# Full-size tail products, full two-batch tiles and all of q loaded ahead, in the ramp of a fused linear attention and two expert layers

## The chip, the cores and the metric

The kernel runs on one core of a Trainium2 chip, in one launch. The time is that of the device from start to end, in microseconds (us), as the median of several runs. One more execution was taken with the hardware profiler; its rows are the ones shown below. PE is TensorE, the matrix engine; DVE is VectorE, ACT is ScalarE, POOL is GpSimd, and SP is the engine that issues most of the DMA transfers.

## What is computed

```python
# q, k, v: (4, 8, 576, 64), float32
kv = np.einsum('bhsd,bhse->bhde', k, v)
out = np.einsum('bhsd,bhde->bhse', q, kv)
rms = np.sqrt(np.mean(out * out, axis=-1, keepdims=True) + 1e-06)
x = (out / rms * g_norm)            # then as 2304 tokens of 512
# first layer, 512 -> 2048 -> 512
h = np.maximum(x @ w_in, 0.0)
x = h * h @ w_out
# second layer, four experts of 1024
p = domain_probs / (domain_probs.sum(-1, keepdims=True) + 1e-09)
for e in range(4):
    out2 += p[:, e:e + 1] * (np.maximum(x @ w1[e], 0.0) @ w2[e])
```

Attention here has no softmax: for each head, a 64 x 64 matrix kv is summed over the 576 positions of its batch, and each token's q is multiplied by it. w_in and w_out come as 64-bit numbers.

## The kernel before

**Tiles.** Two heads share one product of 128 x 128, of which only the two 64 x 64 blocks on the diagonal are wanted. There are 4 batches x 4 head pairs, so 16 such products, called k0 to k15 (batch 0 has k0 to k3, and so on). A batch has 576 = 4 x 128 + 64 positions: four full chunks of 128 rows and a tail of 64. The 2304 tokens make 18 tiles of 128; since 576 is 4.5 tiles, tiles 4 and 13 hold tokens of two batches. The tokens are also taken in five blocks, of 512, 512, 512, 512 and 256 (`BLK`, `j` in the code).

**Units of work.** The program is a list of named units, run through in order; each writes its instructions for all engines. `RAMP` is the hand-written list for the attention and the start of the first layer; `rest()` makes the list behind it.

- `k` (`att_kv`): PE multiplies k and v of a pair, four full chunks (L286) and then the tail (L287), which lies on half of the 128 rows of its tile. The two blocks are copied to a matrix `kvd`, which is zero elsewhere, one by ACT (L289) and one by DVE (L290). It then issues the load of the pair eight further on. There are eight `kvd`, so k8 writes over that of k0.
- `o` (`att_a`, `att_out`): PE multiplies a tile of q by the four `kvd` of its batch (L301). A tile with two batches does so in two halves of 64 tokens. ACT squares the result (L310), DVE sums the squares of each head (L311).
- `c` (`att_c`): DVE and ACT make the factors 1/rms for a group of two or three tiles (L325 to L330), and DVE multiplies the products by them into `xn` (L333).
- `b` (`att_b`): PE transposes `xn` (L344); ACT scales it by g (L348) and rounds it to `hi` (L148), POOL makes the low part `lo` (L149). Both stand in `x`, one tile for each block. Products of the layers are sums of three products of such parts.
- `w` (`split_w`, `narrow`) takes the next piece of weights and loads the one two further on into the freed place (there are two). Each slice of the first layer has four pieces; the first four are called w0 to w3 here. ACT takes an absolute value (L173), DVE takes five steps (L175, L179, L182, L187, L188). `y` (`split_narrowed`) lets ACT round (L231) and POOL do two operations (L232, L233).
- `f` (`g1`): a slice's first product of the layer for a block (L377); ACT then takes ReLU (L382), the square (L384) and the rounding, POOL the low part. `g` (`g2a`) is the second product (L398), which DVE adds up in an accumulator `acc`, one for each block.

**Order.** Each engine works through its own list of instructions in order; a framework builds these lists from the units and may set independent instructions of different units in another order. An instruction waits on semaphores for what it reads, and for the last use of the place that it writes. Products on PE go to eight banks. A float32 product of 128 x 128 shows as two passes (rows "x8" for four chunks).

**Places and loads.** SP issues the loads in its order; the framework has eight semaphores for DMA transfers, so a transfer waits until that eight before it has landed. k and v of the first six pairs go to places that later are the accumulators of blocks 1 to 3, the others to two places of their own; tails have two places, tiles of q four. Loads for later pairs and tiles are issued as places come free.

Of the kernel before, what the change touches and what calls it, by code (L numbers as in the profile page):

```python
# [43 lines left out]


# [75 lines left out]
def fused_kernel(ctx, tc, kvm, kvt, qt, g2, probs, w64, w32, out):  # L121
# [170 lines left out]

    def att_out(t, ss):
        po = ps.tile([P, 512], F32, tag="ps", name=f"po{t}")
        q = q_in.pop(t)
# [12 lines left out]
        load_q(t + NQ)  # L308
        sq = tmp.tile([P, 512], F32, tag="tmp", name=f"sq{t}")
        nc.scalar.activation(out=sq, in_=po, func=AF.Square)  # L310
# [1 line left out]
        return po
# [7 lines left out]
    def att_c(g):  # L320
# [10 lines left out]
        for m, t in enumerate(group):  # L331
            xn = tmp.tile([P, 512], F32, tag="tmp", name=f"xn{t}")
            nc.vector.tensor_tensor(  # L333
                out=xn.rearrange("p (h d) -> p h d", h=H),
                in0=po_t.pop(t).rearrange("p (h d) -> p h d", h=H),
                in1=st[:, 3, m, :].unsqueeze(2).to_broadcast([P, H, D]), op=ALU.mult,
            )
# [224 lines left out]
    with ExitStack() as actx:  # L562
# [11 lines left out]
        load_kv(0)
        load_kv(1)
        load_w(0)
        load_kv(2)
        load_kv(3)
        load_q(0)
        load_q(1)  # L580
        load_w(1)
        load_q(2)
        load_q(3)
# [55 lines left out]
```

## Time and profile before

| | |
|---|---|
| median of 3 runs | 1217.11 us (1216.68 to 1217.98) |
| profiled execution | 1214.15 us |
| its span | 1212.4 us |
| PE busy | 1193.0 us, 98% |
| DVE busy | 765.8 us, 63% |
| POOL busy | 500.3 us, 41% |
| ACT busy | 439.9 us, 36% |

The span runs from the first to the last instruction of the profiled execution. Busy time is that of instructions alone, without waits. PE is the bound over most of the span; in the first 50 us the DMA engines and DVE are as busy as PE is. In that stretch a time line by engine tells more than a sum: what an instruction waits for is in square brackets behind it.

### The profile page before, as it was taken

The page shows a single profiled execution, that of the slowest core. Times are in us where ns is not written, and L with a number is a line of the kernel's source. Part 1 is how long each engine was busy: PE and PEld are TensorE (multiplying, and loading weights), DVE is VectorE, ACT ScalarE, POOL GpSimd, SP SyncE. Part 2 cuts the span into 40 slices and gives each one's busy share as a digit, 9 for nine tenths or more (in the row PEclk, how much of TensorE's full clock was granted, in tenths as well). Part 3 has the DMA queues.
Part 4 walks back from the last instruction along what each step waited for, and adds up shares of the span by engine and source line. Part 5 has one row for each costly group of instructions (what it writes and reads, how often), then busy time and mean ns, then how long its engine had stood idle before and what let it go on. Part 6 is the DMA issues. An engine that isn't in the chain of part 4 may idle for free.

```text
span 1212.4 us, 14974 instructions
## 1 busy us (share of the span) xinstructions
PE 1193.0 (98%) x5768; PEld 1003.2 (83%) x5768; DVE 765.8 (63%) x1177; ACT 439.9 (36%) x798; POOL 500.3 (41%) x390
## 2 busy tenths in 40 slices
PE   7999999999999999999999999999999999999998
PEld 6888788888888888888888888888788888888887
DVE  5968845545546466566666566656876666666655
ACT  4575444434445563222222222322433232323220
POOL 3556635445546675222323222323645242434310
PEclk9999999999999999999999999999999999999999
DMA  8611201111111101110111101111131121111101
GB/s 317 233 42 53 88 18 53 35 36 53 44 44 45 59 20 33 37 36 35 36 53 35 52 35 35 36 52 35 52 123 70 35 70 35 67 38 63 42 1 70
DMA packets 22247, 70.20 MB, mean 58 GB/s; under 512 B 2720, under 2 KB 2720, under 8 KB 22176
## 3 DMA queue, kind: packets, MB, share of 16 engines
q1 hardware_dynamic: 21888, 69.22, 16.7%
q8 instruction: 45, 0.74, 0.2%
q14 instruction: 26, 0.21, 0.1%
q10 hardware_dynamic: 288, 0.04, 0.0%
HBM read 64.52 MB, written 4.72 MB: 57 GB/s over the span
## 4 chain that ended last, share of the span: by engine, by line
PE 91%; DVE 5%; DMA 1%; issue 1%; POOL 1%; ACT 1%; SPq 0%; DVEq 0%; POOLq 0%; ACTq 0%
PE p L529 32%; PE p L377 18%; PE p L398 15%; PE pa L484 7%; PE pd L484 7%; PE pc L484 7%; PE pb L484 4%; PE po L301 1%; DVE u L179 1%; DMA kvs<-in_kvm 1%; DVE u L182 1%; DVE k L188 1%; DMA raw<-in_w 1%; DVE u L175 0%; PE pt L344 0%
## 5 line engine op out<-in xcount | busy, mean ns | idle before, releaser
L529 PE MATMUL p<-b,hh 128*128 128x512 f32 x1152 | 382.8, 390 | 0.5 <-ACT hh L516 0.5
L529 PEld LDWEIGHTS p<-b,hh 128*128 128x128 f32 x1152 | 216.3, 188 | 45.0 <-ACT hh L516 0.7
L539 DVE SCALAR_TENSOR_TENSOR acc<-p,p_sb,acc 128x512 f32<-128x512 f32 x270 | 199.4, 745 | 49.7 <-PE p L529 49.1
L529 PE MATMUL p<-b,hl 128*128 128x512 f32 x576 | 224.6, 390 | 0.0
L377 PE MATMUL p<-x,a 128*128 128x512 f32 (+1 forms) x960 | 204.3, 368 | 0.0
L377 PEld LDWEIGHTS p<-x,a 128*128 128x128 f32 x960 | 167.7, 189 | 30.4 <-PE po L301 0.2
L398 PE MATMUL p<-hh,b 128*128 128x512 f32 (+1 forms) x640 | 189.7, 370 | 0.0
L149 POOL TENSOR_TENSOR a<-raw,a 128x512 fp32r<-128x512 f32 x64 | 85.6, 1338 | 232.8 <-DVE pd L511 149.0
L405 DVE TENSOR_TENSOR acc<-p,acc 128x512 f32<-128x512 f32 (+1 forms) x140 | 87.9, 633 | 142.6 <-PE p L398 141.7
L149 POOL TENSOR_TENSOR b<-raw,b 128x512 fp32r<-128x512 f32 x64 | 82.1, 1303 | 188.0 <-ACT b L148 186.7
L149 POOL TENSOR_TENSOR hl<-s,hh 128x512 fp32r<-128x512 f32 (+1 forms) x80 | 97.9, 1226 | 120.0 <-ACT hh L148 116.7
L398 PEld LDWEIGHTS p<-hh,b 128*128 128x128 f32 x640 | 116.5, 189 | 20.2 <-ACT hh L148 0.4
L529 PEld LDWEIGHTS p<-b,hl 128*128 128x128 f32 x576 | 108.2, 188 | 21.4 <-DVE hl L517 0.2
L398 PE MATMUL p<-hl,b 128*128 128x512 f32 (+1 forms) x320 | 118.3, 370 | 2.4 <-POOL hl L149 2.4
L484 PE MATMUL pc<-o,a 128*128 128x512 f32 x384 | 97.6, 390 | 2.1 <-DVE u L499 2.1
L484 PE MATMUL pa<-o,a 128*128 128x512 f32 x384 | 97.6, 389 | 0.0
L484 PE MATMUL pd<-o,a 128*128 128x512 f32 x384 | 97.4, 389 | 0.0
L149 POOL TENSOR_TENSOR a<-w,a 128x512 fp32r<-128x512 f32 x64 | 85.0, 1328 | 25.3 <-ACT a L148 25.3
L148 ACT ACTIVATE a<-raw 128x512 fp32r<-128x512 f32 x64 | 40.1, 629 | 140.6 <-DMA raw<-in_w 109.2
L382 ACT ACTIVATE r<-p 128x512 f32<-128x512 f32 (+1 forms) x80 | 44.1, 552 | 122.2 <-PE p L377 121.7
L484 PEld LDWEIGHTS pc<-o,a 128*128 128x128 f32 x384 | 72.0, 188 | 17.5 <-DVE u L499 2.5
L484 PEld LDWEIGHTS pd<-o,a 128*128 128x128 f32 x384 | 72.1, 188 | 15.0
(92 smaller groups left out, 1477.3 us busy)
## 6 DMA issues: line engine op xcount, KB each, us to landing
raw<-in_w SPq DMA_DIRECT2D x96, 512.0 KB, 3.7
kvm<-in_kvm SPq DMA_DIRECT2D x10, 512.0 KB, 4.0
q<-in_qt SPq DMA_DIRECT2D x18, 256.0 KB, 4.6
out<-acc SPq DMA_DIRECT2D x18, 256.0 KB, 3.5
kvs<-in_kvm SPq DMA_DIRECT2D x6, 512.0 KB, 7.2
kvt<-in_kvt SPq DMA_DIRECT2D x4, 256.0 KB, 6.0
p_raw<-in_probs ACTq DMA_DIRECT2D x1, 36.0 KB, 4.8
g_sb<-in_g ACTq DMA_DIRECT2D x1, 0.5 KB, 4.3
```

Source lines behind the costliest of these rows:

```text
L148: nc.scalar.activation(out=hi, in_=full, func=AF.Copy)
L149: nc.gpsimd.tensor_tensor(out=lo, in0=full, in1=hi.bitcast(F32), op=ALU.subtract)
L179: nc.vector.scalar_tensor_tensor(out=u, in0=high, scalar=0xC0000000, in1=u, op0=ALU.bitwise_and, op1=ALU.bitwise_or)
L182: nc.vector.scalar_tensor_tensor(out=u.bitcast(F32), in0=k, scalar=1.125 * 2.0**-15, in1=u.bitcast(F32), op0=ALU.is_ge, op1=ALU.mult,)
L188: nc.vector.scalar_tensor_tensor(out=k.bitcast(F32), in0=low, scalar=2.0**-52, in1=k.bitcast(F32), op0=ALU.mult, op1=ALU.mult)
L377: nc.tensor.matmul(pt[:, :n], w, x, start=(i == 0), stop=(i == len(steps) - 1))
L382: nc.scalar.activation(out=r[:, :n], in_=pt[:, :n], func=AF.Relu)
L398: nc.tensor.matmul(pt[:, :n], w, h, start=(i == 0), stop=(i == len(steps) - 1))
L405: nc.vector.tensor_tensor(out=a, in0=pt[:, :n], in1=a, op=ALU.add)
L484: nc.tensor.matmul(pr[bank], x, y, start=(m == 0 and not more), stop=(m == len(steps) - 1), skip_group_check=more,)
L529: nc.tensor.matmul(pt, h, w, start=(i == 0), stop=(i == len(steps) - 1))
L539: nc.vector.scalar_tensor_tensor(out=a, in0=pt, scalar=pe, in1=a, op0=ALU.mult, op1=ALU.add)
```

## The change

- **Loads.** All of k, v of pairs 0 to 9 and all of q are loaded ahead, in the order of a new list `LOADS`. k and v of the first eight pairs go to two places that later are `x` of blocks 2 and 3; q goes to the five accumulators' places. The later pairs still have two places of their own.
- **Tails.** The tail of a batch is one tile of 128 rows for all four pairs, of which the lower 64 rows are set to zero once by POOL; the load fills the upper 64. The tail's product is a full one. There are two such tiles; that of batch b + 2 is loaded behind the last pair of batch b.
- **Two-batch tiles.** Tiles 4 and 13 are multiplied in full by the `kvd` of each of their two batches, into two banks; squares and `xn` take 64 rows from each.
- **Copies.** Both blocks of `kvd` are copied by ACT.
- **Order.** The first `w` and `y` of `RAMP` stand behind k3 and o1, no longer ahead of k0 and behind k1.

```diff
+LOADS = """
+k0 k1 q0 k2 k3 w0 q1 q2 q3 w1 k4 q4 k5 q5 k6 q6 k7 q7 k8 q8 k9 q9 q10 q11 q12 q13 q14 q15 q16 q17
+""".split()
 RAMP = """
-w k0 k1 y k2 k3 o0 o1 k4 c0 o2 o3 b0 k5 k6 b1 c1 b3 w b2 k7 y w o4 o5 y k8 o6 w k9 f0.0.0 y
+k0 k1 k2 k3 w o0 o1 y k4 c0 o2 o3 b0 k5 k6 b1 c1 b3 w b2 k7 y w o4 o5 y k8 o6 w k9 f0.0.0 y
...
-    NQ = 4
+    NKV = 2
+    stage = [xp.tile([P, 4, 2, NCK, P], F32, tag="xs", name=f"kvs{i}", bufs=4) for i in range(2)]
+    NSTAGE = 8
...
+    def load_tails(b):
+        if b < B:
+            nc.sync.dma_start(out=tails[b % 2][:STAIL], in_=kvt[b])
     def load_kv(i):
...
-        if c == 0:
-            tails[b] = attp.tile([P, 2, 2, P], F32, tag="kvt", name=f"kvt{b}")
-            nc.sync.dma_start(out=tails[b], in_=kvt[b])
+        if c == 0 and b < 2:
+            load_tails(b)
...
-        q_in[t] = attp.tile([P, NPAIR, P], F32, tag="q", name=f"q{t}", bufs=NQ)
-        nc.sync.dma_start(out=q_in[t], in_=qt[t])
+        j, m = divmod(t, 4)
+        if m == 0:
+            q_in[j] = accp.tile([P, BLK[j][1] // P, NPAIR, P], F32, tag=f"acc{j}", name=f"q{j}")
+        nc.sync.dma_start(out=q_in[j][:, m], in_=qt[t])
     def att_kv(i):
...
-        tl = tails[b][c % 2 * STAIL : (c % 2 + 1) * STAIL, c // 2]
+        tl = tails[b % 2][:, c]
...
         nc.scalar.activation(out=kd[:D, :D], in_=pk[:D, :D], func=AF.Copy)
-        nc.vector.tensor_copy(kd[D:, D:], pk[D:, D : 2 * D])
-        load_kv(i + NSTAGE + 2)
+        nc.scalar.activation(out=kd[D:, D:], in_=pk[D:, D:P], func=AF.Copy)
+        if i >= NSTAGE:
+            load_kv(i + NKV)
+        if c == NPAIR - 1:
+            load_tails(b + 2)
     def att_out(t, ss):
...
         while done < P:
             b, r = divmod(t * P + done, S)
-            n = min(P - done, S - r)
+            rows = slice(done, done + min(P - done, S - r))
+            po = ps.tile([P, 512], F32, tag="ps", name=f"po{t}_{b}")
             for c in range(NPAIR):
                 nc.tensor.matmul(
-                    po[done : done + n, c * P : (c + 1) * P],
-                    q[:, c, done : done + n],
-                    kvd[(b * NPAIR + c) % NKVD],
+                    po[:, c * P : (c + 1) * P], q[:, c, :], kvd[(b * NPAIR + c) % NKVD],
                     start=True, stop=True,
                 )
-            done += n
-        load_q(t + NQ)
-        nc.scalar.activation(out=sq, in_=po, func=AF.Square)
+            nc.scalar.activation(out=sq[rows], in_=po[rows], func=AF.Square)
+            parts.append((rows, po))
+            done = rows.stop
...
+        tails += [small.tile([P, NPAIR, 2, P], F32, name=f"kvt{i}", bufs=1) for i in range(2)]
+        for t in tails:
+            nc.gpsimd.memset(t[STAIL:], 0.0)
```

`att_c` multiplies each of a tile's parts by its rows of the factors; the identity for the transposes is made behind the memsets.

The lists of two engines differ at one place between k8 and f0.0.1. In the names below, `pk8` is the product of k8, `po6_1` that of tile 6, `p1_0_0_0` and `p1_0_0_1` are f0.0.0 and f0.0.1, `k0_2` and `k0_3` the absolute values of w2 and w3, `sq4` the squares of tile 4, `b0` and `a0` the rounded weights. On PE, before:

```order
L286 MATMUL pk8_394<-kvm8_166 128x128 x4
L287 MATMUL pk8_394<-kvt2_168 128x128
L301 MATMUL po6_403<-kvd4_97,q6_252 128x128
L301 MATMUL po6_403<-kvd5_98,q6_252 128x128
L301 MATMUL po6_403<-kvd6_99,q6_252 128x128
L301 MATMUL po6_403<-kvd7_100,q6_252 128x128
L286 MATMUL pk9_423<-kvm9_178 128x128 x4
L287 MATMUL pk9_423<-kvt2_168 128x128
L377 MATMUL p1_0_0_0_433<-x0_80,a0_146 128x512 x12
L377 MATMUL p1_0_0_1_455<-x0_80,a0_146 128x512 x12
```

and after:

```order
L298 MATMUL pk8_384<-kvm8_147 128x128 x4
L320 MATMUL po6_1_396<-kvd4_99,q1_139 128x128
L320 MATMUL po6_1_396<-kvd5_100,q1_139 128x128
L320 MATMUL po6_1_396<-kvd6_101,q1_139 128x128
L320 MATMUL po6_1_396<-kvd7_102,q1_139 128x128
L298 MATMUL pk9_413<-kvm9_151 128x128 x4
L395 MATMUL p1_0_0_0_425<-x0_82,a0_197 128x512 x12
L395 MATMUL p1_0_0_1_447<-x0_82,a0_197 128x512 x12
L299 MATMUL pk8_384<-kvt0_103 128x128
L299 MATMUL pk9_413<-kvt0_103 128x128
```

The two tails (L287, now L299) have moved behind f0.0.0 and f0.0.1. On ACT, at the same place, before:

```order
L231 ACTIVATE a0_146<-u0_1_326 128x512
L173 ACTIVATE k0_2_356<-raw0_2_156 128x512
L310 ACTIVATE sq4_378<-po4_367 128x512
L310 ACTIVATE sq5_388<-po5_381 128x512
L289 ACTIVATE kvd0_93<-pk8_394 64x64
L231 ACTIVATE b0_147<-u0_2_358 128x512
L310 ACTIVATE sq6_410<-po6_403 128x512
L289 ACTIVATE kvd1_94<-pk9_423 64x64
```

and after:

```order
L240 ACTIVATE a0_197<-u0_1_319 128x512
L301 ACTIVATE kvd0_95<-pk8_384 64x64
L302 ACTIVATE kvd0_95<-pk8_384 64x64
L301 ACTIVATE kvd1_96<-pk9_413 64x64
L302 ACTIVATE kvd1_96<-pk9_413 64x64
L182 ACTIVATE k0_2_348<-raw0_2_207 128x512
L324 ACTIVATE sq4_359<-po4_0_360 64x512
L324 ACTIVATE sq4_359<-po4_1_366 64x512
L324 ACTIVATE sq5_373<-po5_1_374 128x512
L240 ACTIVATE b0_198<-u0_2_350 128x512
```

The copies from `pk8` and `pk9`, now two each, stand ahead of the absolute value of w2 (L173, now L182) and of the squares. On SP, the loads around w2 (`raw0_2`), before:

```order
L268 DMA kvm6_142<-in_kvm 128x1024
L268 DMA kvm7_144<-in_kvm 128x1024
L164 DMA raw0_2_156<-in_w64 128x512
L271 DMA kvt2_168<-in_kvt 128x512
L268 DMA kvm8_166<-in_kvm 128x1024
```

and after:

```order
L278 DMA kvm9_151<-in_kvm 128x1024
L290 DMA q2_149<-in_qt 128x512 x3
L290 DMA q3_156<-in_qt 128x512 x4
L290 DMA q4_161<-in_qt 128x512 x2
L268 DMA kvt0_103<-in_kvt 64x1024
L173 DMA raw0_2_207<-in_w64 128x512
L173 DMA raw0_3_325<-in_w64 128x512
```

w2 has moved behind k9, the last nine tiles of q and the tail of batch 2.

## Rows read from the trace of the kernel before

**Rows 1.** The page: busy time, share of the span, instructions.

```profile
PE 1193.0 (98%) x5768; PEld 1003.2 (83%) x5768; DVE 765.8 (63%) x1177; ACT 439.9 (36%) x798; POOL 500.3 (41%) x390
```

**Rows 2.** What PE waited for: us in total, times, longest.

```profile
PE pk L286 <- DMA kvs<-in_kvm: 6.1, 2, 5.0
PE po L301 <- DVE kvd L290: 2.6, 2, 1.9
...
PE pc L484 <- DVE u L499: 2.1, 1, 2.1
```

**Rows 3.** PE's time line: start, busy us, operation, count, wait.

```profile
4.96 2.07 PE L286 MATMUL pk<-kvs 128*128 128x128 f32 x8 [4.96 <-DMA kvs<-in_kvm]
...
26.15 1.06 PE L286 MATMUL pk<-kvm 128*128 128x128 f32 x8
27.14 0.48 PE L287 MATMUL pk<-kvt 64*128 64x128 f32 x2
27.55 1.36 PE L301 MATMUL po<-kvd,q 128*64 128x128 f32 x14
...
34.80 5.74 PE L377 MATMUL p<-x,a 128*128 128x512 f32 x24
40.38 1.05 PE L286 MATMUL pk<-kvm 128*128 128x128 f32 x8
...
58.17 2.05 PE L301 MATMUL po<-kvd,q 128*128 128x128 f32 x16
...
64.36 1.58 PE L301 MATMUL po<-kvd,q 128*64 128x128 f32 x16
65.88 5.75 PE L377 MATMUL p<-x,a 128*128 128x512 f32 x24
...
73.72 1.95 PE L301 MATMUL po<-kvd,q 128*128 128x128 f32 x16
75.50 0.60 PE L344 MATMUL pt<-ident,xn 128*128 128x128 f32 x4
```

**Rows 4.** The chain that ended last, first 17 us: start, us, what.

```profile
2.10 6.34 DMA raw<-in_w
...
8.46 7.82 DMA kvs<-in_kvm
```

**Rows 5.** DVE's time line in the ramp, columns as for PE.

```profile
34.63 0.68 DVE L182 SCALAR_TENSOR_TENSOR u<-k,u 128x512 f32<-128x512 f32 x1
...
36.52 1.70 DVE L188 SCALAR_TENSOR_TENSOR k<-raw,k 128x512 f32<-128x512 uint32 x1
...
44.15 0.69 DVE L188 SCALAR_TENSOR_TENSOR k<-raw,k 128x512 f32<-128x512 uint32 x1
44.88 1.29 DVE L333 TENSOR_TENSOR xn<-po,st 128x512 f32<-128x512 f32 x2
...
46.45 1.28 DVE L311 TENSOR_REDUCE st<-sq 128x8 f32<-128x512 f32 x2
...
61.94 1.47 DVE L188 SCALAR_TENSOR_TENSOR k<-raw,k 128x512 f32<-128x512 uint32 x1
```

**Rows 6.** POOL's time line: last additions of w1 and of slice 1's first piece.

```profile
32.22 1.33 POOL L233 TENSOR_TENSOR a<-u,k 128x512 fp32r<-128x512 f32 x1
...
63.56 1.28 POOL L233 TENSOR_TENSOR a<-u,k 128x512 fp32r<-128x512 f32 x1 [0.69 <-DVE st L325]
64.80 1.26 POOL L149 TENSOR_TENSOR x<-xg,x 128x512 fp32r<-128x512 f32 x1
```

**Rows 7.** ACT's time line: the absolute value of w2, the copy from pk8.

```profile
29.36 0.66 ACT L173 ACTIVATE k<-raw 128x512 f32<-128x512 f32 x1
...
32.52 0.22 ACT L289 ACTIVATE kvd<-pk 64x64 f32<-64x64 f32 x1 [0.71 <-PE pk L287]
```

**Rows 8.** The kvd copies (L290) on DVE in 34.63 to 63.41: busy, granted clock.

```profile
34.63:63.41 28.78, 1.59 (x7) 1.00 0.69 233
```

**Rows 9.** What DVE waited for between 34.6 and 63.45 us.

```profile
DVE st L311 <- ACT sq L310: 0.9, 1, 0.9
```

More of the change, by code (lines that the diff above doesn't have):

```diff
@@ L133, in fused_kernel @@
     NKVD = 2 * NPAIR
-    NQ = 4
-    kvd = []
+    NKV = 2
+    kvd, tails = [], []
     p_sb = const.tile([P, NTT, E], F32, name="p_sb")
+    stage = [xp.tile([P, 4, 2, NCK, P], F32, tag="xs", name=f"kvs{i}", bufs=4) for i in range(2)]
+    NSTAGE = 8
     x_t = [
@@ L252, in operands @@
             split(*(a[:, x, 2:4] for x in range(2)), st[n])
-    kv_in, q_in, tails, stage, st_t, po_t, att_mid = {}, {}, {}, [None], {}, {}, {}
-    NSTAGE = 6
+    kv_in, q_in, st_t, po_t, att_mid = {}, {}, {}, {}, {}
+    def load_tails(b):
+        if b < B:
+            nc.sync.dma_start(out=tails[b % 2][:STAIL], in_=kvt[b])
     def load_kv(i):
@@ L262, in load_kv @@
         if i < NSTAGE:
-            if i % 2 == 0:
-                stage[0] = accp.tile([P, 2, 2, NCK, P], F32, tag=f"acc{i // 2 + 1}", name=f"kvs{i}")
-            m = stage[0][:, i % 2]
+            m = stage[i // 4][:, i % 4]
         else:
-            m = attp.tile([P, 2, NCK, P], F32, tag="kvm", name=f"kvm{i}")
+            m = attp.tile([P, 2, NCK, P], F32, tag="kvm", name=f"kvm{i}", bufs=NKV)
         nc.sync.dma_start(out=m, in_=kvm[b, c])
-        if c == 0:
-            tails[b] = attp.tile([P, 2, 2, P], F32, tag="kvt", name=f"kvt{b}")
-            nc.sync.dma_start(out=tails[b], in_=kvt[b])
+        if c == 0 and b < 2:
+            load_tails(b)
         kv_in[i] = m
@@ L289, in att_kv @@
         nc.scalar.activation(out=kd[:D, :D], in_=pk[:D, :D], func=AF.Copy)
-        nc.vector.tensor_copy(kd[D:, D:], pk[D:, D : 2 * D])
-        load_kv(i + NSTAGE + 2)
+        nc.scalar.activation(out=kd[D:, D:], in_=pk[D:, D:P], func=AF.Copy)
[3 more added lines that the diff above has]
+            load_tails(b + 2)
     def att_out(t, ss):
-        po = ps.tile([P, 512], F32, tag="ps", name=f"po{t}")
-        q = q_in.pop(t)
+        q = q_in[t // 4][:, t % 4]
+        sq = tmp.tile([P, 512], F32, tag="tmp", name=f"sq{t}")
+        parts = []
         done = 0
@@ L298, in att_out @@
             b, r = divmod(t * P + done, S)
[L299 removed]
+            rows = slice(done, done + min(P - done, S - r))
+            po = ps.tile([P, 512], F32, tag="ps", name=f"po{t}_{b}")
             for c in range(NPAIR):
                 nc.tensor.matmul(
[L302 to L304 removed]
+                    po[:, c * P : (c + 1) * P], q[:, c, :], kvd[(b * NPAIR + c) % NKVD],
                     start=True, stop=True,
                 )
[L307 to L310 removed]
+            nc.scalar.activation(out=sq[rows], in_=po[rows], func=AF.Square)
+            parts.append((rows, po))
+            done = rows.stop
         nc.vector.reduce_sum(ss, sq.rearrange("p (h d) -> p h d", h=H), axis=mybir.AxisListType.X)
[L312 removed]
+        return parts
     def att_a(t):
@@ L332, in att_c @@
             xn = tmp.tile([P, 512], F32, tag="tmp", name=f"xn{t}")
[L333 to L337, printed above, removed]
+            for rows, po in po_t.pop(t):
+                nc.vector.tensor_tensor(
+                    out=xn[rows].rearrange("p (h d) -> p h d", h=H),
+                    in0=po[rows].rearrange("p (h d) -> p h d", h=H),
+                    in1=st[rows, 3, m, :].unsqueeze(2).to_broadcast([rows.stop - rows.start, H, D]),
+                    op=ALU.mult,
+                )
             att_mid[t] = xn
@@ L556, in fused_kernel @@
     )
+    load = dict(k=load_kv, q=load_q, w=load_w)
     ext = None
@@ L573, in fused_kernel @@
         nc.scalar.activation(out=warm, in_=warm, func=AF.Sqrt)
[L574 to L583, printed above, removed]
         nc.scalar.dma_start(out=g_sb, in_=g2)
-        for i in range(4, NSTAGE + 2):
-            load_kv(i)
+        for name in LOADS:
+            load[name[0]](int(name[1:]))
         for name in RAMP:
```

5 lines of the change are left out of this document (2 added, 3 removed).

## The prediction

> **What bounds the kernel now.** I read the page's list of engines first, then the list of what the matrix engine (PE) waited for, then PE's own time line, and last the queues that feed it. PE is busy for 1193.0 us of a span of 1212.4 [rows 1], so almost any time that PE saves or waits is time of the kernel. Its longest waits lie at the front [rows 2]: 6.1 us for the first loads of k and v, 2.6 for kvd copies on DVE. The question for every edit is therefore what it does to the time at which PE reaches a given matmul in the ramp. I take the first group of f0.1.0 as the mark: PE begins it at 65.88 us [rows 3]. All products of k with v, and all of q but four tiles, lie before it, and what follows it on PE is the same work in the same order in both kernels, but for those four. A delay there is a delay of the end, and so is a gain.
>
> **PE's own work.** Four full chunks of one head pair, 8 passes, take 0.99 us (26.15 to 27.14), but the tail of 64 rows takes 0.41 for 2 passes (27.14 to 27.55) [rows 3], where two full passes would take 0.25 at the chunks' pace. The work behind a tail is longer too: 16 passes of q are busy for 2.05 us behind one (58.17) and 1.95 behind other work (73.72) [rows 3]. A full tail so saves 0.16 + 0.10 = 0.26 us, 16 of them 4.2 us. The two tiles with two batches now need 16 full passes, 1.78 us (73.72 to 75.50), instead of 16 half ones, 1.52 (64.36 to 65.88) [rows 3]: 0.26 each, 0.5 together. PE's work falls by 3.7 us. [...] All of this work lies before the mark, so it counts only if PE, and not something it waits for, sets the time of the mark.
>
> **The loads.** The loads land at an even pace here: three MiB, from the landing of the first weights (w0, 8.46 us) to that of k4 (16.28), took 7.82 us, 2.61 us per MiB [rows 4]. In the new order 3.0 MiB end with w0 instead of 1.75, so w0 lands at 8.46 + 1.25 x 2.61 = 11.7 us. k4 still ends 4.75 MiB, at 16.3. The third piece of weights, w2, now stands behind all 18 tiles of q, k8, k9 and a tail: 11.75 MiB, so 8.46 + 10 x 2.61 = 34.6 us. Before, DVE was at its third step on w2 at 34.63 [rows 5]. On the queue of SP, which issues these loads, the tail of batch 2 now stands ahead of w2 and waits for the last product of batch 0; that is done some 20 us earlier. w3 and k10, queued behind, come by 38 us and are needed later.
>
> **The first 33 us.** DVE takes w0 apart later, but k4 arrives when it did. With PE, DVE and GpSimd (POOL) walked through from these landings with the durations of the trace, I get the second pair of xn within 0.4 us of before and the end of DVE's work on w1 within 0.3. The kvd copies that leave DVE bring little here: by this walk DVE then meets POOL's additions instead. POOL's last addition for w1 ended at 33.55 before [rows 6], and I keep that. PE is ready for f0.0.0 at about 33.1, since it leaves the tails of pk8 and pk9 for later; it begins at about 33.5 instead of 34.80 [rows 3]. So far PE has 1.3 us in hand.
>
> **Where the time goes: ACT's queue.** The new order puts the tails of pk8 and pk9 on PE behind f0.0.0 and f0.0.1, and on ACT the four copies from pk8 and pk9 ahead of the absolute value of w2, the squares of tiles 4 to 6 and everything for w3. ACT works through its list in order (its rows in the trace stand as in the list), so all of these wait for f0.0.1. Before, the copy from pk8 ran at 32.52 and the absolute value of w2 had been done since 29.36 [rows 7]. After: f0.0.0 and f0.0.1 take 5.58 less the 0.10 behind a tail (34.80 to 40.38) [rows 3], to 39.0; two tails to 39.45; ACT's four copies of 0.22 end at 40.2, the absolute value, 0.66, at 40.9 [rows 7]. DVE's third step on w2 starts at 40.9 instead of 34.63: 6.3 us late. That w2 itself lands at 34.6 doesn't matter; it has 5 us to spare. [...]
>
> **What DVE makes good.** From this step to the end of the first piece of weights of slice 1 (61.94 + 1.47 = 63.41) [rows 5], DVE is busy for almost all of 28.78 us. Of this it loses seven kvd copies, 1.59 us [rows 8], and 0.9 us in which it waited for a square [rows 9], which will be there early. It gains a reduction that used to stand ahead of this stretch (half of 1.28) and the second half of xn4 (half of 1.29) [rows 5]; an instruction over 64 partitions with as many columns I price like a full one. A half price would give back 0.3 us. So 28.78 - 1.59 - 0.9 + 0.64 + 0.64 = 27.6, and it ends at 68.5 instead of 63.4: 5.1 us late. POOL follows with the second addition (63.56) and only then the low part of x for tile 6 (64.80) [rows 6], without which f0.1.0 can't go past its first pass. From the end of f0.0.1 to the mark PE took 25.5 us (40.38 to 65.88) [rows 3], 1.9 of it one wait [rows 2]; without that, with six tails cheaper and one tile dearer, some 22.3 are left, so from 39.5 PE could be there at 62. It is not the bound, and its 3.7 us buy nothing. f0.1.0 moves by 5.1 us.
>
> **What costs nothing.** ACT takes a second copy of 0.22 us for each of 16 pairs, 3.5 us on an engine that is busy for 36% of the span [rows 1]; where they stand in front of something is priced above. The two memsets on POOL only have to be done when the first tail runs, at about 7 us (4.96 + 2.07) [rows 3], and were they late, each microsecond would count, since PE has nothing else. q in the places of the accumulators, and k and v in those of x, are read by PE long before PE makes what is written there, so nothing waits for them.
>
> **The unknown size: DVE against POOL.** The same DVE step takes 0.69 us when it runs free (44.15) and 1.70 when POOL is at work at its start (36.52) [rows 5]. In the stretch of 28.78 us five DVE instructions were so held, 3.8 us in all. Which will be held after the change depends on tenths of a microsecond. With none, the mark moves by 5.1 - 3.8 = 1.3 us; with twice as much, by 8.9. I take the same sum as before, since the same steps meet the same POOL additions; my walk, with the small steps of c2 now between those for w3, gave 7.1, so the upper half is no less likely than the lower.
>
> **The sum.** 5.1 us on the profiled execution's 1214.15 us (its span is 1212.4) is 1219.2. The median of the runs is 1217.11, 2.96 above that execution, so I state 1217.1 + 5.1 = 1222.2.
>
> **Rivals.** (1) DVE is hardly held: 1218.4, no difference that can be measured. For it: fewer DVE instructions. Against it: POOL's work is unchanged and all five held steps are still there.
> (2) Faster: PE's saving comes through. This needs the wait on ACT to be gone, which it is if f0.0.1 is done by the time that w2 lands: f0.0.0 would have to start at about 29 us, 4.5 earlier than POOL's last addition for w1 allows in [rows 6]. Each microsecond nearer to it gives back one, and past 4.5 the full 3.7 us are gained: 1217.1 - 3.7 = 1213.4. For it: DVE no longer waits for a copy from pk7 ahead of its last step on w1. Against it: POOL has the additions for tiles 2 and 3 to do ahead of those for w1, and they follow xn as before.
> [...]
>
> **How the numbers follow.** Forecast, 1222.2: 0.65. Rival 3: 0.15, also slower. Rival 1: 0.13. Rival 2: 0.07. A measurement here can tell about 0.2% from no change, so faster means under 1214.7 and slower over 1219.5. Faster 0.07, same 0.13, slower 0.80. The range of 8 in 10 runs from 1217.8, just under the case without held steps, to 1226.5: 8.9 us for twice the held time is 1226.0, and a little of rival 3. Left out are rival 2 and what lies above both.
>
> **What would show each step.** In the trace after: single tails of about 0.25 us; w2 landing near 34.6; f0.0.0 at 33 to 34; the absolute value of w2 on ACT at 40 to 41, right behind four copies; DVE's third step on w2 there; PE waiting several microseconds for ACT's ReLU and for xn4; f0.1.0 at about 71. If that absolute value runs before 36, the forecast's cause is wrong. If it runs at 40 and f0.1.0 still starts by 67, DVE makes good more than I grant it. If the mark moves by 5 and the total doesn't, something behind the ramp gives the time back.

## The result, and the profile after

The changed kernel takes 1228.23 us (median of 4 runs, 1225.02 to 1230.08) against 1217.55 of the kernel before: a ratio of 1.0084, 95% interval 1.0060 to 1.0107. A second set of runs gave 1228.80 against 1216.70, 1.0100 (1.0081 to 1.0120). So it is slower, as forecast, but by 11 to 12 us instead of 5.1, and above the range, which ended at 1226.5. The runs of before spread over 1214.1 to 1219.5, and both of its profiled executions (1214.15 and 1214.47) are among the shortest, while the profiled execution of after (1230.08) is the longest of its four. A difference of two traces can therefore come out 2.5 us or more above that of the medians: here it is 15.9 us by the traces and 10.7 by the medians.

The page of the kernel after, its line of engines, for [rows 1]; PE's busy time has risen by 6.2 us, although its work fell:

```profile
PE 1199.2 (98%) x5768; PEld 1012.1 (82%) x5768; DVE 761.8 (62%) x1163; ACT 445.0 (36%) x816; POOL 500.9 (41%) x392
```

What PE waited for after, for [rows 2]: us in total, times, longest.

```profile
PE pk L298 <- DMA kvs<-in_kvm: 7.7, 3, 5.0
PE pt L362 <- DVE xn L350: 7.7, 3, 3.0
...
PE po L320 <- ACT r L400: 2.1, 1, 2.1
PE pk L298 <- ACT r L400: 2.1, 1, 2.1
PE pk L298 <- DMA kvm<-in_kvm: 1.0, 1, 1.0
```

PE's time line after, for [rows 3]: start, busy us, operation, count, wait.

```profile
17.46 1.45 PE L298 MATMUL pk<-kvs 128*128 128x128 f32 x8 [2.26 <-DMA kvs<-in_kvm]
...
22.65 1.06 PE L298 MATMUL pk<-kvs 128*128 128x128 f32 x8
23.54 0.39 PE L299 MATMUL pk<-kvt 128*128 128x128 f32 x2
23.77 1.06 PE L298 MATMUL pk<-kvs 128*128 128x128 f32 x8
...
36.56 5.72 PE L395 MATMUL p<-x,a 128*128 128x512 f32 x24
42.11 0.61 PE L299 MATMUL pk<-kvt 128*128 128x128 f32 x4
...
57.01 1.11 PE L362 MATMUL pt<-ident,xn 128*128 128x128 f32 x4 [3.03 <-DVE xn L350]
...
77.00 5.50 PE L395 MATMUL p<-x,a 128*128 128x512 f32 x23 [0.31 <-POOL x L158]
...
95.40 0.66 PE L362 MATMUL pt<-ident,xn 128*128 128x128 f32 x4 [2.51 <-DVE xn L350]
```

A tail now takes 0.23 us (23.54 to 23.77), as expected. k4 comes at 17.46, f0.0.0 at 36.56, and the two tails of pk8 and pk9 stand behind it (42.11). The mark, the start of f0.1.0, is at 77.00 instead of the 71.0 that were forecast. Its group (f0.1.0 and f0.1.1) ends at 77.00 + 5.50 = 82.50, before at 65.88 + 5.75 = 71.63: 10.9 us late. And there is a wait that the forecast didn't have, for xn13 at 95.40. The ACT and DVE lines at the place on which the forecast rested, for [rows 5] and [rows 7]:

```profile
42.54 0.22 ACT L301 ACTIVATE kvd<-pk 64x64 f32<-64x64 f32 x1 [9.90 <-PE pk L299]
...
43.48 0.67 ACT L182 ACTIVATE k<-raw 128x512 f32<-128x512 f32 x1
```

```profile
40.19 0.43 DVE L184 TENSOR_SCALAR u<-raw 128x512 uint32<-128x512 uint32 x1 [7.77 <-DMA raw<-in_w]
40.65 0.69 DVE L188 SCALAR_TENSOR_TENSOR u<-raw,u 128x512 uint32<-128x512 uint32 x1
44.17 0.69 DVE L191 SCALAR_TENSOR_TENSOR u<-k,u 128x512 f32<-128x512 f32 x1 [2.83 <-ACT k L182]
...
72.81 1.49 DVE L197 SCALAR_TENSOR_TENSOR k<-raw,k 128x512 f32<-128x512 uint32 x1
```

ACT waits 9.9 us for the tails, makes its four copies, and takes the absolute value of w2 at 43.48; DVE's third step follows at 44.17, and the stretch that begins there ends at 74.30. That is the forecast's mechanism. But w2 itself landed only at 40.19. Last, the windows of five us: busy time of PE, PEld, DVE, ACT and POOL, then granted clock of PE, DMA share, GB/s (before, the clock is 1.00 in all of them):

```profile
15.00:20.00 5.00, 2.74 (x16) 2.41 (x16) 4.62 (x10) 1.68 (x6) 2.52 (x2) 0.82 1.04 349
...
50.00:55.00 5.00, 2.50 (x10) 2.21 (x10) 5.00 (x10) 4.74 (x12) 2.94 (x2) 0.50 0.63 203
55.00:60.00 5.00, 2.99 (x14) 3.00 (x15) 4.00 (x9) 1.18 (x4) 2.48 (x2) 0.50 0.59 205
95.00:100.00 5.00, 4.60 (x16) 3.73 (x17) 3.68 (x10) 1.35 (x3) 2.05 (x2) 0.67 0.00 0
```

From 50 to 60 us the granted clock is 0.50, and in the window behind the wait at 95.40 it is 0.67.

### The profile page after: what moved, and what is told of

The parts are those of the page before. It is cut to its first block, busy times and chain, and to the rows that moved or that the text cites. A ratio compares the mean times of both kernels' runs of the same rounds, so it can differ in the third digit from the quotient of the medians.

```text
span 1228.3 us, 14984 instructions
## 1 busy us (share of the span) xinstructions
PE 1199.2 (98%) x5768; PEld 1012.1 (82%) x5768; DVE 761.8 (62%) x1163; ACT 445.0 (36%) x816; POOL 500.9 (41%) x392
## 4 chain that ended last, share of the span: by engine, by line
PE 91%; DVE 4%; DMA 2%; issue 1%; POOL 1%; ACT 1%; SPq 0%; DVEq 0%; POOLq 0%; ACTq 0%
PE p L547 32%; PE p L395 18%; PE p L416 15%; PE pc L502 7%; PE pa L502 7%; PE pd L502 7%; PE pb L502 4%; PE po L320 1%; DMA kvs<-in_kvm 1%; DMA kvm<-in_kvm 1%; PE pt L362 1%; DVE u L188 1%; DVE k L197 1%; DVE u L191 1%; DMA q<-in_qt 1%
## 5 line engine op out<-in xcount | busy, mean ns | idle before, releaser
L502 PEld LDWEIGHTS pa<-o,a 128*128 128x128 f32 x384 | 72.4, 189 | 15.1
```

Source lines behind the costliest of these rows:

```text
L502: nc.tensor.matmul(pr[bank], x, y, start=(m == 0 and not more), stop=(m == len(steps) - 1), skip_group_check=more,)
```

## The experiments

All in one table. "f0.1 ends" is the end of the group of f0.1.0 and f0.1.1 in the trace, "to f0.3" the time from there to the start of f0.3.0; behind that all kernels take the same (span less start of f0.3.0 is 1119 to 1120 us in each).

| run | median us | before, same chip | ratio (95%) | f0.1 ends | to f0.3 |
|---|---|---|---|---|---|
| before | | | | 71.63 | 21.63 |
| e9 before again | 1216.21 | 1216.70 | 0.9998 (0.9984 to 1.0013) | 71.97 | 21.62 |
| after | 1228.23 | 1217.55 | 1.0084 (1.0060 to 1.0107) | 82.50 | 25.92 |
| e12 after again | 1228.80 | 1216.70 | 1.0100 (1.0081 to 1.0120) | 81.49 | 25.96 |
| e1 tails spread | 1228.82 | 1215.65 | 1.0107 (1.0088 to 1.0125) | 81.16 | 25.94 |
| e2 four tail places | 1224.97 | 1215.65 | 1.0074 (1.0059 to 1.0089) | 77.37 | 25.97 |
| e3 late q | 1223.74 | 1215.65 | 1.0062 (1.0043 to 1.0080) | 77.13 | 25.98 |
| e4 half tiles | 1222.30 | 1215.65 | 1.0054 (1.0038 to 1.0070) | 79.89 | 21.64 |
| e5 two-batch alone | 1219.12 | 1216.82 | 1.0016 (1.0004 to 1.0028) | 72.50 | 25.91 |
| e6 tails alone | 1215.06 | 1216.82 | 0.9984 (0.9973 to 0.9994) | 71.66 | 21.63 |
| e7 fill | 1231.76 | 1216.82 | 1.0119 (1.0101 to 1.0136) | 87.47 | 23.90 |
| e8 reordered loads | 1217.60 | 1216.82 | 1.0002 (0.9990 to 1.0013) | 74.32 | 21.63 |
| e10 fill b4, b13 | 1227.75 | 1216.70 | 1.0090 (1.0071 to 1.0109) | 83.12 | 23.88 |
| e11 e8 and k10 | 1216.24 | 1216.70 | 1.0000 (0.9990 to 1.0010) | 74.25 | 21.64 |
| e13 fill k11, b13 | 1226.24 | 1216.61 | 1.0078 (1.0060 to 1.0097) | 81.02 | 23.89 |
| e14 copies alone | 1213.12 | 1216.61 | 0.9970 (0.9958 to 0.9982) | 70.59 | 21.60 |
| e15 tails spread on before | 1214.79 | 1216.61 | 0.9985 (0.9976 to 0.9995) | 73.56 | 21.60 |
| e16 e15 and copies | 1213.38 | 1216.61 | 0.9976 (0.9967 to 0.9985) | 70.41 | 21.62 |
| e17 loads alone | 1224.66 | 1215.31 | 1.0082 (1.0054 to 1.0111) | 80.89 | 21.63 |

The last two columns split the loss: ahead of f0.1's end 9.9 to 10.9 us, and 4.3 us behind it. These 4.3 stand in every run that works the two-batch tiles out in full and in no other; in the three runs that fill PE's waits (e7, e10, e13) they are 2.3.

### Ahead of f0.1: the block of tails, the late w2, the tails' loads

**e1**, tails on every second partition of their tiles:

```diff
-            nc.sync.dma_start(out=tails[b % 2][:STAIL], in_=kvt[b])
+            nc.sync.dma_start(out=tails[b % 2][::2], in_=kvt[b])
...
-            nc.gpsimd.memset(t[STAIL:], 0.0)
+            nc.vector.memset(t, 0.0)
```

> The changed kernel, with the rows of a tail on every second partition of its tile (0, 2, 4, ...) instead of on the upper 64; the other partitions are zero (set by DVE at the start). Same bytes, same order on PE, ACT and SP. Theory (a load onto 64 neighbouring partitions goes at half the pace): each tail's load gives back about 0.65 us, so k4 lands near 16.2 instead of 17.46 and w2 near 37.6 instead of 40.19; f0.0.0 starts about 1.2 us earlier, near 35.3; the tails of pk8 and pk9 still stand behind it, so the time falls by about 1.2 us only, to 1227. Rival (the tiles of q between, with their smaller pieces, slow the loads): k4 stays at 17.4 and the time at 1228.2.

The window of 15 to 20 us in e1, and DVE's first step on w2:

```profile
15.00:20.00 5.00, 3.51 (x29) 3.29 (x29) 4.05 (x7) 2.73 (x7) 1.64 (x2) 1.00 1.03 409
```

```profile
37.11 0.43 DVE L184 TENSOR_SCALAR u<-raw 128x512 uint32<-128x512 uint32 x1 [3.64 <-DMA raw<-in_w]
```

With the DMA engines as busy as before (1.03 to 1.04), 409 GB/s are moved instead of 349, and w2 lands 3.1 us earlier, so loads onto 64 neighbouring partitions do go more slowly. These windows hold other loads too; in windows of 0.5 us after moved 180 and 221 GB/s from 16.5 to 17.5 us, at DMA shares of 0.89 and 1.13, where before moved 393 and 401: about the half pace of the theory. k4 didn't gain (17.91), since the first tail's load now waited for DVE's memset; e17 shows it clean. Against e12, the second execution of after, w2 lands 2.3 us earlier (39.45 there). The end of f0.1 gains 1.3 us on after but only 0.3 on e12, and the medians gain nothing. f0.0.0 started at 35.51, although the second pair of xn came when it did in after (26.28 and 26.20): PE's granted clock was 1.00 here from 15 to 45 us, in after 0.82 to 0.84 from 15 to 35. From the second pair of transposes to f0.0.0 e1 took 7.8 us and after 8.9, so by this one pair of traces the low clock cost some 1 us there.

**e2**, four places for tails, the last two loaded behind q7 and q8:

```diff
-k0 k1 q0 k2 k3 w0 q1 q2 q3 w1 k4 q4 k5 q5 k6 q6 k7 q7 k8 q8 k9 q9 ...
+k0 k1 q0 k2 k3 w0 q1 q2 q3 w1 k4 q4 k5 q5 k6 q6 k7 q7 t2 k8 q8 t3 k9 q9 ...
...
-        if c == NPAIR - 1:
-            load_tails(b + 2)
```

> The changed kernel with four places for tails, those of batches 2 and 3 loaded behind q7 and q8. The tails of pk8 and pk9 then stand on PE ahead of f0.0.0 again, and the four copies on ACT come early; w2 is still behind all of q. Theory (both the block of tails and copies and the late w2 hold DVE, one barely behind the other): w2 lands at about 40, its absolute value follows at once, DVE's third step on it starts near 41.7 instead of 44.17, the time falls by 2.5 us to 1225.7. Rival (the block alone holds DVE, as forecast): third step by 36, time near 1219. Rival (PE's low clock sets the time): no change, 1228.

DVE in e2:

```profile
39.68 0.43 DVE L184 TENSOR_SCALAR u<-raw 128x512 uint32<-128x512 uint32 x1 [6.13 <-DMA raw<-in_w]
...
40.94 0.69 DVE L191 SCALAR_TENSOR_TENSOR u<-k,u 128x512 f32<-128x512 f32 x1
```

The block is gone, and the third step comes 3.2 us earlier, not the 8 of the rival by which the block alone holds DVE: then it waits for w2 itself. Both held DVE, the second 3.2 us behind the first.

**e3**, the last nine tiles of q loaded as earlier ones are used (which takes the block away as well):

```diff
-... k7 q7 k8 q8 k9 q9 q10 q11 q12 q13 q14 q15 q16 q17
+... k7 q7 k8 q8 k9
...
+        load_q(t + 9)
         nc.vector.reduce_sum(ss, ...
```

> The changed kernel with the last nine tiles of q not ahead but each loaded as a tile nine earlier is used. w2 so has 2.25 MiB less ahead of it, and the tails of pk8 and pk9 stand ahead of f0.0.0. Theory: w2 lands near 34, DVE's third step on it starts at 36 to 37 instead of 44.17, and the time falls by about 7 us, to 1221. Rival (PE's low clock, or the two-batch tile at 95 us, makes most of the loss): 1225 or more.

DVE's third step on w2 comes at 36.42, 7.8 us earlier than after. But f0.1 ends only 5.4 us earlier, since PE now waits for k10. PE in e3, then the queue of SP:

```profile
47.90 2.04 PE L298 MATMUL pk<-kvm 128*128 128x128 f32 x8 [5.30 <-DMA kvm<-in_kvm]
```

```profile
40.66 0.33 SPq L173 DMA_DIRECT2D raw<-in_w  x1
41.04 0.90 SPq L290 DMA_DIRECT2D q<-in_qt  x2
42.04 0.38 SPq L278 DMA_DIRECT2D kvm<-in_kvm  x1
```

The load of k10 is issued only at 42.04. It stands in SP's list behind w4's (`raw`), which needs the place of w2 and so DVE's last step on it (done at 40.59), and behind two of the tiles of q that were put off. The median, 1223.74, lies between the theory (1221) and the rival (1225 or more).

**e17**, the loads alone, on the kernel before: its tails (packed on 128 partitions), its half tiles and its copy on DVE, with the new `LOADS`, places and order.

> The kernel before with one part of the change only: the loads, their places and the order of the first w and y. Tails are packed on 128 partitions and multiplied as 64 rows, tiles 4 and 13 in halves, the second copy of each kvd on DVE. Two tail places, so the tails of pk8 and pk9 stand behind f0.0.0 on PE and their copies ahead of the absolute value of w2 on ACT. Theory (the loads are nearly the whole loss, and the other parts take off or add little): k4 lands near 16.4, w2 near 37, since these tails' loads go at the full pace; f0.1.0 near 74, time 1223 to 1227. Rival (the parts only cost together): 1220 or less.

PE and DVE in e17, then what DVE waited for between 34 and 76 us:

```profile
16.63 1.16 PE L298 MATMUL pk<-kvs 128*128 128x128 f32 x8 [0.49 <-DMA kvs<-in_kvm]
...
75.12 5.77 PE L393 MATMUL p<-x,a 128*128 128x512 f32 x24
```

```profile
DVE kvd L302 <- ACT kvd L301: 10.0, 1, 10.0
```

The loads alone make f0.1 9.3 us late and the kernel 9.3 us slower: they are most of the loss. That includes the late w0, the late w2 and the block of tails. k4 comes at 16.63, since these tails take all partitions, and PE's clock is 1.00 from 15 to 25 us; f0.0.0 is late all the same (37.21). The wait at the block is not quite that of after: here DVE too has a copy from pk8 in its list ahead of w2's steps, and stands for 10.0 us.

### Behind f0.1: the two-batch tiles

**e4**, the changed kernel with half tiles, and **e5**, the kernel before with full ones:

```diff
-                    po[:, c * P : (c + 1) * P], q[:, c, :], kvd[(b * NPAIR + c) % NKVD],
+                    po[rows, c * P : (c + 1) * P], q[:, c, rows], kvd[(b * NPAIR + c) % NKVD],
...
-            nc.scalar.activation(out=sq[rows], in_=po[rows], func=AF.Square)
+        nc.scalar.activation(out=sq, in_=po, func=AF.Square)
```

> The changed kernel with tiles 4 and 13 multiplied in two halves of 64 tokens into one bank, with one square and one xn each, as before the change. The block of tails stays. Theory (the two parts of tile 13 hold ACT and DVE and so PE, which waits 2.5 us for xn13 at 95.4): that wait goes, and the slower passes behind it, and 0.5 us of PE's passes: 1224.5 to 1226; the start of f0.1.0 moves by under 0.5 us. Rival (that wait only passes on the lateness of the stretch before): within 0.5 us of 1228.2.

> The kernel before with one part of the change only: tiles 4 and 13 multiplied in full for each of their batches, with two squares and two parts of xn each. On DVE the second part of xn13 so stands behind the reduction of tile 16, which waits for PE. Theory (this part alone makes a wait of PE for xn13, after which its clock falls): PE waits about 2.5 us for xn13 near 83 us, the passes behind it take about 1.3 us longer, xn4 takes 0.7 us longer on DVE; in all 4 to 5.5 us over before. Rival (in the kernel after, that wait only passed on lateness from the stretch before, DVE has time in hand here): within 1 us of before.

DVE in e5, the factors behind c5, then PE:

```profile
80.97 0.67 DVE L334 TENSOR_TENSOR xn<-po,st 64x512 f32<-64x512 f32 x1
83.95 0.69 DVE L311 TENSOR_REDUCE st<-sq 128x8 f32<-128x512 f32 x1 [2.30 <-ACT sq L307]
84.66 1.42 DVE L334 TENSOR_TENSOR xn<-po,st 64x512 f32<-64x512 f32 x2
```

```profile
85.42 0.66 PE L346 MATMUL pt<-ident,xn 128*128 128x128 f32 x4 [2.51 <-DVE xn L334]
...
88.12 3.66 PE L379 MATMUL p<-x,a 128*128 128x512 f32 x12
```

And DVE in e4:

```profile
87.70 0.68 DVE L325 TENSOR_REDUCE st<-sq 128x8 f32<-128x512 f32 x1
88.30 0.68 DVE L348 TENSOR_TENSOR xn<-po,st 128x512 f32<-128x512 f32 x1
91.34 0.69 DVE L325 TENSOR_REDUCE st<-sq 128x8 f32<-128x512 f32 x1 [2.36 <-ACT sq L324]
```

And DVE in before, ahead of it:

```profile
80.03 0.68 DVE L333 TENSOR_TENSOR xn<-po,st 128x512 f32<-128x512 f32 x1
83.07 0.69 DVE L311 TENSOR_REDUCE st<-sq 128x8 f32<-128x512 f32 x1 [2.37 <-ACT sq L310]
```

In e4, as in before, the last xn of the group is one instruction and done ahead of the reduction that waits for the square of tile 16, so that wait of DVE costs PE nothing. In two parts, the second stands in DVE's list behind that reduction, 2.3 us later, and b13 on PE needs both. The passes behind it are slow too: 12 passes in 3.66 us, against 2.90 in before. So the wait for xn13 and the slow passes behind it are shown from both sides: gone in e4, made in e5. The sizes fit less well. e4's f0.1.0 comes 1.6 to 2.7 us earlier than in the two executions of after (74.34 against 75.97 and 77.00), where the theory had under 0.5, and its time, 1222.30, lies under the theory's range: the two-batch tiles cost something ahead of the mark too, 0.9 us in e5 to 2.6 in e4. e5's medians show 2.3 us, between rival (up to 1) and theory (4 to 5.5); its trace shows 0.9 + 4.3.

### PE's clock

**e7, e10, e13** put products that nobody reads into PE's waits. In e7 and e10 those at o8 to b4 themselves waited for a bank that ACT or DVE had still to read; so ahead of f0.1 these two made things worse (87.47 and 83.12, where after and e12 have 82.50 and 81.49) and tell nothing. e13 fills from k11's own bank:

```diff
+        pad(pk, PADS.get(f"k{i}", 0), 512)
         for n in range(NCK):
...
+PADS = dict(k11=6, b13=9)
```

> The changed kernel with products whose results are overwritten or never read, put on PE into four of its waits: ahead of o8, k11, b4 and b13 (10, 10, 12 and 9 of them, of 384 to 512 columns, 0.2 us each at the high level). They keep PE at work, so the granted clock should stay at 1.00 from 45 to 100 us. Theory (PE's low clock is hidden by DVE's lateness up to the mark, but not behind b13): f0.1.0 passes its first pass within 0.7 us of 77.0, the passes behind b13 lose 1.2 us, the time falls by 1 to 2 us to about 1226.7. Rival (the low clock makes the mark late): f0.1.0 2 to 3 us earlier and the time near 1223.

> The changed kernel with products whose results are overwritten put on PE into two of its waits only: 7 ahead of b4, 9 ahead of b13, of 512 columns, into the bank that the transposes then write. Theory (PE's low clock behind b4 makes the square of tile 10 late, for which DVE waits 1.9 us; and behind b13 it costs 1.4 us): the granted clock is near 1.00 from 57 us on, f0.1.0 passes its first pass 1 to 1.5 us before 77.0, the passes behind b13 give 1.4 us, the time falls by 2 to 3 us, to 1225.5. Rival (DVE's own steps set the mark): f0.1.0 stays at 77.0, the time falls by 1.4 us at most.

> The changed kernel with products whose results are overwritten put on PE ahead of k11 (6 of them, into its own bank) and of b13 (9), of 512 columns. They take the time in which PE else waits for xn4, so that it should come to b4 at the high level. Theory (PE's low clock behind b4 makes the square of tile 10 late for DVE, and so the mark): the granted clock is 1.00 from 57 us on, the 16 passes and transposes from b4 on take 1.5 us less, f0.1.0 passes its first pass 0.7 to 1.5 us earlier than the 76.0 to 77.0 of the two executions of after; behind b13 2.0 us are saved; time 1225 to 1226. Rival (DVE's own steps set the mark): f0.1.0 within 0.3 us of 76 to 77, time 1226.5 or more.

The windows of e13:

```profile
55.00:60.00 5.00, 2.40 (x20) 2.02 (x19) 4.38 (x11) 1.38 (x5) 1.98 (x2) 1.00 0.56 188
95.00:100.00 5.00, 5.00 (x26) 4.13 (x25) 3.56 (x9) 2.73 (x5) 1.29 (x1) 1.00 0.00 0
```

The clock is 1.00 from 55 us on. Behind f0.1 each of the three fills saves 2.0 us (23.9 instead of 25.9): that is the low clock's part of the 4.3, the rest is the wait. Ahead of it, f0.1 ends 0.5 us earlier than in e12 and 1.5 earlier than in after; 0.24 and 0.58 of this stand already at DVE's third step on w2 (43.59 instead of 43.83 and 44.17). So the 10 us at a clock of 0.50 cost 0.2 to 0.9 us there, and DVE's lateness hides most of what they slow down. The time, 1226.24, falls between theory (up to 1226) and rival (1226.5 or more), and so does the mark.

### The parts that cost nothing

**e6**, full tails on the kernel before; **e14**, both copies on ACT; **e15**, e6 with the tails of batches 1 to 3 on every second partition; **e16**, e15 with e14's edit, which is this line:

```diff
-        nc.vector.tensor_copy(kd[D:, D:], pk[D:, D : 2 * D])
+        nc.scalar.activation(out=kd[D:, D:], in_=pk[D:, D:P], func=AF.Copy)
```

> The kernel before with one part of the change only: tails as full products on tiles whose lower 64 rows are zero (set by DVE at the start), loaded onto the upper 64. Four such tiles here. Theory (PE is not the bound ahead of the mark, and the two first tail loads take twice as long): PE's single tails fall from 0.41 to 0.25 us, but f0.1.0 starts within 1.5 us of 65.88 and the time stays within 1.5 us of before. Rival (PE's saved work counts): up to 4.2 us faster.

> The kernel before with one part of the change only: both copies of each kvd on ACT. Theory (free on ACT, and PE's waits for the copies on DVE, 0.7 and 1.9 us, go): f0.1.0 0.5 to 1.5 us before 65.88, since DVE loses seven copies of 0.23 us in the stretch; time up to 1.5 us under before. Rival (DVE meets GpSimd instead): no change.

> The kernel before with full tails as in e6, those of batches 1 to 3 on every second partition of their tiles, so that their loads should not go at half the pace. Theory: k4 lands at 16.3 instead of 16.95, PE's later wait for a tile of q (2.3 us in e6) shrinks; time 1214 to 1215. Rival (half pace is not from the partitions): as e6, k4 at 16.95.

> e15 with both copies of each kvd on ACT: the two parts of the change that cost nothing by themselves, together. Theory: PE waits for no copy, DVE loses 1.6 us in the stretch; f0.1.0 at 64.5 to 65.5, time 1213 to 1214.5. Rival (DVE meets GpSimd instead, the mark stays): 1214.5 to 1215.5.

PE in e6, and in e14:

```profile
66.14 5.52 PE L376 MATMUL p<-x,a 128*128 128x512 f32 x23 [0.84 <-POOL x L149]
```

```profile
47.87 0.49 PE L301 MATMUL po<-kvd,q 128*128 128x128 f32 x2 [0.87 <-ACT kvd L290]
...
64.85 5.74 PE L377 MATMUL p<-x,a 128*128 128x512 f32 x24
```

In e6 PE saves work but waits 0.84 us for POOL at the mark, and the group ends where it ended before (71.66 and 71.63). It does so although f0.0.0 began 3.9 us later than before (38.67), so PE doesn't set that time. The medians are 1.8 us lower, by an interval that lies just clear of 1; no trace shows where that comes from, and before has runs above 1217 that e6 doesn't have. e15 comes out as e6 in the medians (its k4 at 17.20, so nothing of the expected gain at the front is seen). e14 moves the mark by 1.0 us and the median by 3.5 (0.9970, 0.9958 to 0.9982). **It is faster than both kernels**; the tails add nothing to it (e16). Its profiled execution is only 1.1 us shorter than that of before, in line with the mark; the other 2.5 us of the medians are the distance of before's runs from its own trace, which no run explains.

**e8 and e11** put together what is left of the change when its costly parts go: half tiles, four tail places, w0 third again, w2 ahead of the last ten tiles of q; in e11 also places for k10 and k11.

> The changed kernel without what was found to cost: tiles 4 and 13 in halves; four places for tails; loads in the order of before at the front (w0 third), w2 ahead of the last ten tiles of q, the first w and y of the list in their old places. Left of the change: full tails, both copies on ACT, k, v and q in the new places. Theory (late w0 and w2, the block of tails and the two-batch tiles are all of the loss): f0.1.0 starts within 1 us of 65.88, the time is 1213 to 1217, at most 0.2% from before. Rival (copies on ACT or the loads of tails cost too): 1219 or more.

> As e8, and k and v of pairs 10 and 11 have places of their own, so that they are loaded ahead too; the tails of batches 1 to 3 lie on every second partition. Theory (the wait of 4.2 us for pair 10, behind all late loads, and the low clock after it are what e8 still loses): k10 doesn't wait, DVE's wait of 4.3 us for a square goes, f0.1.0 passes its first pass at 65 to 66.5, the time is 1213 to 1215. Rival (DVE and GpSimd hold each other as before, whatever PE does): 1216 to 1218.

Both are level with before. In e8 PE waits 4.2 us for k10, as in e3; in e11 that wait is gone, yet f0.1 ends at the same time: the absolute value of w3 on ACT now holds DVE for 3.4 us. But e16, which has the same full tails and the same copies on the old loads, takes 1213.38: against that, loading ahead still costs about 3 us in these two orders.

**e9 and e12**, both kernels once more. e12's waits on PE are those of after within 0.4 us. In e9 three of the five waits of before behind the first differ by 0.8 to 1.5 us (1.80 against 0.32, for example), and still f0.1 ends within 0.4 us of before.

> The kernel before once more, for a second profiled execution of it: the first took 1214.15 us, at the low end of its runs (1214.2 to 1219.5, median 1216.8). Theory (the runs differ in the ramp, by waits of PE of a few tenths to 2.5 us that come or go with the landing of a load): an execution above 1216 shows a wait of PE for kvd or xn that the first doesn't, or a lower granted clock behind one. Rival (they differ outside the span, or evenly over it): the same waits within 0.3 us.

> The changed kernel once more, beside the others on one chip, for a second profiled execution (the first took 1230.08 us, the longest of four). Theory: w2 lands near 40, f0.1.0 passes its first pass near 77, PE waits 2.5 us for xn13; median 1227 to 1229. Rival (the late w2 or the wait for xn13 were of that execution): median unchanged, but one of the two is missing from the trace.

In e12 w2 lands at 39.45, and the waits of 3.0 us for xn4 and 2.51 for xn13 are there again. Why some runs of before take up to 5 us more stays open: neither of its profiled executions was such a one, and what it does to the medians stands in each difference from before.

## Why the prediction was right and wrong

The mark was forecast at 71.0 and stands at 77.00. Of these 6.0 us, 3.1 are there at f0.0.0 (36.56 instead of 33.5), 0.2 come in ACT's queue, 2.5 in the stretch that DVE sets, and 0.2 from there to the mark. Behind the mark 4.3 us are added where the forecast has none. So the traces miss the forecast by 10 us and the medians only by 6: the forecast carried over before's 3 us from its profiled execution to its median, and after's median lies 1.9 us under its profiled execution.

**Right: the ACT queue.** From the start of f0.0.0 to DVE's third step on w2 the forecast had 7.4 us (33.5 to 40.9), the trace has 7.6 (36.56 to 44.17), in the order that was forecast: f0.0.1, tails, four copies, absolute value, DVE.

**Right by the traces: PE's own work buys nothing.** Tails take 0.23 us; in e6 the group at the mark ends where it did. The 1.8 us by which e6's median is lower stay open.

**Wrong: "The loads".** 2.61 us per MiB came from rows in which nearly every transfer went to 128 partitions. The tails' loads, now on 64, go more slowly: that is 0.8 of the 1.2 us by which k4 came late (17.46 against 16.3; 16.63 in e17) and 2.3 to 3.1 of the 5.6 us of w2 (40.19 against 34.6; 39.45 in e12, 37.11 in e1). The rest of w2, 2.5 us, is not settled; w3 and a tail are issued right behind it, and no run shows what they do to it. From 15 to 20 us, with such loads among others, 349 GB/s were moved in after and 409 in e1, where the tails lie on every second partition. The forecast prices the matmuls of the tails by their own rows and their loads by the pace of other transfers, though the same edit moved both.

**Wrong: "w2 has 5 us to spare".** It had 3 (44.17 - 40.65 less a step), and e2 shows that behind the block it was the next to wait for.

**Wrong: "The first 33 us".** The forecast had the second pair of xn within 0.4 us of before, and 1.3 us in hand at f0.0.0. The pair came 2.4 us later than before, and f0.0.0 was 1.8 late (36.56 against 34.80). DVE in after: its first step on w0, its last one, and the second pair of xn; then that pair in before, and in e8, where w0 is loaded third again.

```profile
12.41 0.43 DVE L184 TENSOR_SCALAR u<-raw 128x512 uint32<-128x512 uint32 x1 [5.92 <-DMA raw<-in_w]
16.59 1.67 DVE L197 SCALAR_TENSOR_TENSOR k<-raw,k 128x512 f32<-128x512 uint32 x1
26.20 1.29 DVE L350 TENSOR_TENSOR xn<-po,st 128x512 f32<-128x512 f32 x2
```

```profile
23.82 1.29 DVE L333 TENSOR_TENSOR xn<-po,st 128x512 f32<-128x512 f32 x2
```

```profile
23.93 1.29 DVE L347 TENSOR_TENSOR xn<-po,st 128x512 f32<-128x512 f32 x2
```

The step that failed is the walk of DVE's list: w0, loaded later, is taken apart among the first factors, and these come late. In all ten kernels with w0 in its new place the pair came at 25.6 to 27.0, with w0 loaded third (the eight others, and e9) at 23.7 to 25.3. No run moves w0 alone. k4's lateness and the low clock behind it (o2 and o3 took 3.02 us instead of 2.05) are not what makes the pair late: in e17, with k4 at 16.63 and the clock at 1.00, it came at 26.47. How the 3.1 us at f0.0.0 are made up is less sure. Some 1 us of it is the low clock behind the pair (e1), but f0.0.0 also varies without any of this: with w0 third it started anywhere from 34.7 to 38.7 (e6), with w0 late at 35.5 to 37.2.

**Wrong: "What DVE makes good".** 27.6 us were forecast for the stretch; it took 30.1 in after, 29.4 in e12, 29.2 in e13. In it DVE waited 2.5, 1.8 and 1.6 us for squares, where the forecast set 0 ("which will be there early"). Without these waits 27.6 us are left in all three, so the rest of that sum came out and the wait is its failed term.

**Wrong: the two-batch tiles.** They were priced at PE's passes and DVE's partitions, with "the same work in the same order" behind the mark. The DVE list had changed there: the second part of xn13 stands behind the reduction of tile 16. The wait (2.3 us) and the low clock behind it (2.0) are the second largest term of the loss, and the forecast has none for it.

**Rival 3, the clock**, stands in the chances with 0.15 and in the upper end of the range: a lower clock of PE behind its wait at b4, put by the author at up to 2.5 us. No run shows that term. The clock did fall, in more places than b4; at b4 that costs 0.2 to 0.9 us, at b13 2.0 us and, by one pair of traces, about 1 ahead of f0.0.0. In after the granted clock was 0.50 to 0.82 in windows of 5 us (15 to 20, 50 to 60, 95 to 100) that held or followed waits of 2.1 to 3.0 us; in e1 it stayed at 1.00 from 25 to 35 us behind a wait of 2.1 (27.72).

**"The kvd copies that leave DVE bring little"** was too low: alone they give the largest gain of all parts, 1.0 us at the mark and 3.5 by the medians (e14).

By the traces the parts nearly add up: loads +9.3 (e17), two-batch tiles +5.2 (e5), copies -1.1 (e14), tails 0.0 (e6), together 13.4, where after has 14.2 (e12) and 15.2. The medians don't add up in this way: +9.3, +2.3, -3.5 and -1.8 are 6.4, where after has 10.7 and 12.1. The 2.5 us by which before's runs lie above its own traces stand in each of these differences, and what makes them stays open.

## What to carry to other kernels

A change of several edits can hold a gain under a loss: try the parts one by one. Here one line of it gained, while the whole lost. When an instruction is split in two, look up in each engine's list where the second half went; when loads are moved ahead, write down what then stands behind them on the same queue, and how many partitions each one reaches. A wait that is taken from one place (the block, q) shows the next one behind it (w2 was 3.2 us behind the block, the absolute value of w3 0.1 us behind k10), so price both before counting on the gain.

## What the runs showed of the hardware

With a load onto 64 neighbouring partitions among the others, a window of 5 us moved 349 GB/s at a DMA share of 1.04; with 128 partitions (e17) or every second one (e1) it moved 400 to 409. A wait of 2.5 us on PE cost 2.0 us more behind it (25.9 instead of 23.9 us from the end of f0.1 to f0.3), with the granted clock at 0.67 from 95 to 100 us (after), and products that only keep PE at work took these 2.0 us away, with the clock at 1.00 (e13). DVE's product for xn over 512 columns took the same time on 64 partitions as on 128, 686 ns, so half the partitions saved nothing (after, by form: busy us in all, mean ns of one):

```profile
L350 DVE TENSOR_TENSOR xn<-po,st 128x512 f32<-128x512 f32 x16 | 10.4, 686 | 0.7
L350 DVE TENSOR_TENSOR xn<-po,st 64x512 f32<-64x512 f32 x4 | 2.7, 686 | 0.6 <-DVE st L346 0.5
```
